# Moving a fused attention and state-space kernel's side work off GpSimd: x in two channel halves, the gate on TensorE, the skip weight in the first tap

## The chip, the cores and the metric

The kernel runs on one core of a Trainium2 chip. The metric is the device time of one execution in microseconds (us). Engines are named as the profile names them: PE (TensorE), ACT (ScalarE), DVE (VectorE), POOL (GpSimd), SP (the queue that issues most DMAs).

## The reference, cut to what matters

```python
x = A_x                                            # (1, 2048, 512), bfloat16
g = sigmoid((x * gate_w).sum(-1, keepdims=True))   # one gate for each row
# a: 32 heads of 16 channels over 2048 rows, softmax attention, then @ wo
# b: for each of 512 channels a causal convolution over 2048 rows with
#    K[d, l] = Re(sum_n C[d,n] * exp(dt*A[d,n])**l * dt*B[d,n]), plus x * Dskip
return g * a + (1 - g) * b
```

Attention needs 32 x 2048 x 2048 exponentials. In the kernel they are 1024 ACT instructions of 128x1024.

## The kernel before: what matters here

A small scheduler writes one fixed program for each engine. The main loop has 512 steps, and a step holds two of the 1024 exponentials (`ET<-SC`). Side work (projections, parameters, the state-space branch) comes from generators that spend a budget of PE and DVE time in each step. **Every engine and the SP queue then run their own list strictly in order**, so an instruction that waits also holds back all that were recorded after it.

```python
for q in range(512):
    ex(2 * q); qk(q + 1); ex(2 * q + 1)     # two exponentials; scores of the next step
    ... pv(q - 1) ...                       # exponentials times V, into OA
    sch.step(rate)                          # side work, as much as the budget allows
```

The stages of the state-space branch share one PSUM bank, `MB`. They run block by block (16 blocks of 32 channels): a table of powers on DVE; K, the first 64 taps; S, the state of every chunk of 64 rows; a scan over the chunks for each quarter of the channels; and y, the output, in 32 units.

```python
def kstage(blk):                             # [...] matmuls PT x weights into MB
    op("DVE", ... Kst(63, ...) <- MB ...)    # ONE Kst
    dma("SP", ... kpd <- Kst ...)
def sstage(blk):                             # after the transposed load Qt<-ptd
    for bank in range(4):
        # 4 matmuls of 128 rows x 64 columns: Ut (x in block form) times Qt, into MB
        op("DVE", ... Sst(512 * (bank % 2), ...) <- MB ...)       # TWO slots
        dma("SP", ... sd <- Sst ...)
def quarter(qr):                             # the scan
    for bl in range(4):
        yield ("AFTER", f"sg{4 * qr + bl}", 4)   # 4 steps after the loads are issued
    # then per chunk: s2 = G*MU; s3 = ...; G = s2 + sg + s3   (all DVE)
def ublocks():                               # x in block form: channel pairs on partitions
    # 8 x  op("POOL", tensor_copy(UB, X2))   64 x 2048 elements each
def gate():
    # 16 x dma xg <- x ;  op("DVE", tensor_tensor_reduce(xg * gw -> gp[lt]))
    # 16 x dma xh <- x ;  op("POOL", xD = xh * Dskip)
for th in (projs(), params(), scan(), bases(), table(), ystage(), ublocks(), gate(), combine(), outs()):
    sch.add(th)                              # priority in this order
```

The softmax here doesn't subtract the row's maximum and nothing guards it: scores larger than these inputs give would overflow.

## Time and profile before

| | before |
|---|---|
| time, median of its runs | 1171.6 us |
| ACT busy | 978.9 us (84%) |
| PE / DVE / POOL busy | 65% / 57% / 6% |
| first exponential | 17.9 us |
| last exponential ends, then tail | 1146.5 us, 22.3 us |

From the page of the kernel before: the busy times, the rows of ACT and of PE's granted clock over 40 slices of the span in tenths, the group of the exponentials, and the group of the POOL copies (busy, mean ns | idle before, and what ended it).

```profile
PE 755.2 (65%) x5997; PEld 204.7 (18%) x6016; DVE 671.8 (57%) x1525; ACT 978.9 (84%) x1039; POOL 64.4 (6%) x36
...
ACT  5456999993798989799879796889799698999992
...
PEclk9767998555556555565655565555555555555568
...
L515 ACT ACTIVATE ET<-SC 128x1024 bf16<-128x1024 f32 x1024 | 965.5, 1104 | 120.0 <-PE SC L422 107.9
...
L926 POOL COPY UB<-X_140 64x2048 bf16<-64x2048 bf16 x8 | 31.4, 3920 | 49.7 <-DMA X_140<-gm_xrd 49.2
```

ACT is the busiest engine. In its timeline, undisturbed stretches run at 0.918 us an exponential (92 in 84.44 us), so 1024 of them need 940 us. The other 229 us of the span are the subject. ACT's row shows them: the first four slices are half empty, many in the middle are at 6 to 8 (one at 3), and the last is at 2. The clock row shows PE at about half clock from about 200 us until near the end (mean 0.85 up to 205 us, 0.52 from there to 1120 us).

The waits view names for each waiter what it waited for: us in total, times, longest.

```profile
ACT ET L515 <- PE SC L422: 107.9, 49, 8.5
...
DVE Sst L778 <- DMA gm_sd<-Sst: 30.5, 12, 4.3
...
DVE G L819 <- DMA SG_136<-gm_sd: 19.5, 2, 17.8
...
ACT ge L945 <- DVE gp L941: 17.6, 1, 17.6
DVE G L819 <- DMA SG_135<-gm_sd: 17.2, 1, 17.2
...
ACT u_101 L607 <- DVE u_99 L540: 9.6, 1, 9.6
ACT u_101 L600 <- DVE u_99 L598: 9.4, 1, 9.4
```

ACT's own line says only that scores came late. Its causes are the lines in which DVE waits for a DMA, because PE needs DVE to empty `MB`, and ACT needs PE. The gate's exponential (`ge`) and the two square roots (`u_101`) waited for DVE directly.

Two stretches of the timeline (start us, duration us, engine, line, what it writes and reads, and in brackets the idle time before it and what ended it). First the head:

```profile
35.62 0.68 DVE L540 TENSOR_TENSOR zi<-u_101,u_102 128x512 f32<-128x512 f32 x1
...
36.74 7.64 POOL L926 COPY UB<-X_140 64x2048 bf16<-64x2048 bf16 x2 [23.95 <-DMA X_140<-gm_xrd]
36.84 4.07 DVE L540 TENSOR_TENSOR u_99<-zr 128x512 f32<-128x512 f32 x1
...
40.84 4.10 DVE L540 TENSOR_TENSOR u_100<-zi 128x512 f32<-128x512 f32 x1
...
46.17 0.63 ACT L600 ACTIVATE u_101<-u_99 128x512 f32<-128x512 f32 x1 [9.39 <-DVE u_99 L598]
```

The same kind of DVE operation takes 0.68 us without a POOL copy beside it and 4.1 us with one. The square root waits 9.4 us for that.

Then a block of the state stage:

```profile
351.40 7.19 SPq L784 DMA_DIRECT2D gm_sd<-Sst  x4
...
355.88 0.42 DVE L778 CAST Sst<-MB 128x256 bf16<-128x256 f32 x1 [4.21 <-DMA gm_sd<-Sst]
...
356.69 0.64 PE L422 MATMUL MB<-Qt,Ut 128*64 128x256 bf16 x4 [4.22 <-DVE Sst L780]
...
357.26 0.61 PE L422 MATMUL SC<-Qm,KT 32*128 32x512 bf16 x4
...
357.91 1.94 ACT L515 ACTIVATE ET<-SC 128x1024 bf16<-128x1024 f32 x2 [4.58 <-PE SC L422]
```

The third `Sst` eviction waits 4.2 us for the store that still reads its slot; then the PE matmuls into `MB` go on, then the scores of the next step, which stand behind them in PE's list, and ACT has been idle for 4.6 us.

### The profile page before, as it was taken

To read this page: it belongs to the slowest core of one execution; us is meant where nothing else is said; L and a number is where in the kernel's file an instruction comes from. 1 tells how busy PE (TensorE), PEld (TensorE's weight loads), DVE (VectorE), ACT (ScalarE), POOL (GpSimd) and SP (SyncE) were. 2 spreads that over 40 slices of the span, in tenths; PEclk is the share of its full clock that TensorE was granted. 3 is DMA by queue.
4 is the path that set the end of the run, shared out by engine and by line. 5 is a ranking of instruction groups with operands and counts; after the bars stand their busy time and mean duration, and the time that the engine had idled before them with its cause. 6 is when DMAs were issued, how large, how long until landed. Compare 5 with 4: busy or idle time off the path is not lost.

```text
span 1168.8 us, 15477 instructions
## 1 busy us (share of the span) xinstructions
PE 755.2 (65%) x5997; PEld 204.7 (18%) x6016; DVE 671.8 (57%) x1525; ACT 978.9 (84%) x1039; POOL 64.4 (6%) x36
## 2 busy tenths in 40 slices
PE   5345766662665656656566775756588467888775
PEld 1111111110111111111111122311133012333111
DVE  5778889965576976589757521129711793011413
ACT  5456999993798989799879796889799698999992
POOL 4442000000000000000000015000000000000000
PEclk9767998555556555565655565555555555555568
DMA  9660000043687018630356635550156203544001
GB/s 217 138 148 36 1 1 1 1 135 99 175 186 189 1 54 199 181 72 1 109 166 163 181 104 141 124 128 1 32 126 122 48 1 93 126 115 112 14 19 49
DMA packets 239176, 111.24 MB, mean 95 GB/s; under 512 B 191616, under 2 KB 222720, under 8 KB 237056
## 3 DMA queue, kind: packets, MB, share of 16 engines
q1 hardware_dynamic: 237376, 108.56, 37.1%
q10 hardware_dynamic: 1728, 1.70, 0.5%
q8 instruction: 47, 0.77, 0.3%
q14 instruction: 25, 0.20, 0.1%
HBM read 42.34 MB, written 39.85 MB: 70 GB/s over the span
## 4 chain that ended last, share of the span: by engine, by line
DVE 35%; ACT 34%; PE 10%; DMA 10%; SPq 6%; issue 2%; POOL 1%; another core or an unknown queue 0%; ACTq 0%; DVEq 0%; POOLq 0%
ACT ET L515 34%; DVE G L829 4%; PE MB L422 4%; DMA gm_sd<-Sst 4%; PE SC L422 4%; DVE s_138 L827 4%; DVE s_138 L822 3%; DVE s_139 L824 3%; PE OA L422 2%; DVE tt_130 L540 2%; DVE PT L540 2%; DMA xg<-in_A_x_dram 2%; DVE tt_131 L540 2%; DVE SG_136 L831 2%; DVE SG_135 L831 2%
## 5 line engine op out<-in xcount | busy, mean ns | idle before, releaser
L515 ACT ACTIVATE ET<-SC 128x1024 bf16<-128x1024 f32 x1024 | 965.5, 1104 | 120.0 <-PE SC L422 107.9
L422 PE MATMUL SC<-Qm,KT 32*128 32x512 bf16 x2048 | 294.9, 566 | 240.4 <-ACT ET L515 225.4
L422 PE MATMUL OA<-ET,VE 128*32 128x512 bf16 x2048 | 292.8, 575 | 13.6 <-DVE OT L530 12.8
L422 PEld LDWEIGHTS SC<-Qm,KT 32*128 32x128 bf16 x2048 | 54.9, 97 | 453.5 <-ACT ET L515 417.9
L890 DVE CAST Yst<-MB 128x256 bf16<-128x256 f32 x32 | 13.4, 420 | 177.0 <-PE MB L422 177.0
L422 PEld LDWEIGHTS OA<-ET,VE 128*32 128x32 bf16 x2048 | 54.0, 101 | 206.9 <-issue 187.0
L422 PE MATMUL MB<-Qt,Ut 128*64 128x256 bf16 x256 | 39.1, 405 | 71.4 <-DVE Sst L780 52.5
L530 DVE STREAM_TRANSPOSE OT<-OA 128x512 f32<-128x512 f32 x32 | 23.8, 744 | 66.9 <-PE OA L422 66.8
L778 DVE CAST Sst<-MB 128x256 bf16<-128x256 f32 x64 | 27.0, 421 | 60.8 <-DMA gm_sd<-Sst 30.5
L829 DVE TENSOR_TENSOR G<-s_138,s_139 128x256 f32<-128x256 f32 x120 | 51.0, 425 | 4.1
L422 PE MATMUL MB<-Tt,Uy 128*64 128x64 bf16 x256 | 33.7, 260 | 29.8 <-DVE Yst L890 15.6
L822 DVE TENSOR_TENSOR s_138<-G,MU 128x256 f32<-128x256 f32 x120 | 50.1, 417 | 0.1
L824 DVE TENSOR_TENSOR s_139<-G,MU 128x256 f32<-128x256 f32 x120 | 50.1, 418 | 0.0
L540 DVE TENSOR_TENSOR PT<-tt_130,tt_131 128x512 bf16<-128x512 bf16 x96 | 40.8, 425 | 3.3
L956 POOL TENSOR_TENSOR xD<-xh,Dsk 128x512 bf16<-128x512 bf16 x16 | 19.6, 1244 | 397.4 <-DMA xh<-in_A_x_dram 397.4
L422 PE MATMUL MB<-xT,Wk 128*128 128x512 bf16 x60 | 21.3, 444 | 26.1 <-DMA xT<-in_A_x_dram 10.4
L926 POOL COPY UB<-X_140 64x2048 bf16<-64x2048 bf16 x8 | 31.4, 3920 | 49.7 <-DMA X_140<-gm_xrd 49.2
L757 DVE CAST Kst<-MB 128x512 bf16<-128x512 f32 x16 | 11.1, 694 | 36.8 <-PE MB L422 36.8
L422 PEld LDWEIGHTS MB<-Tt,Uy 128*64 128x64 bf16 x256 | 16.9, 127 | 83.5 <-issue 67.8
L422 PE MATMUL MB<-Py,SG_136 128*32 128x64 bf16 x512 | 29.9, 314 | 0.0
L422 PE MATMUL MB<-Py,SG_135 128*32 128x64 bf16 x512 | 29.9, 314 | 0.0
L422 PEld LDWEIGHTS MB<-Qt,Ut 128*64 128x64 bf16 x256 | 11.5, 137 | 100.8 <-DVE Sst L780 74.8
(203 smaller groups left out, 647.0 us busy)
## 6 DMA issues: line engine op xcount, KB each, us to landing
gm_ptd<-PT SPq DMA_DIRECT2D x16, 1024.0 KB, 4.0
Py<-gm_ptd SPq DMA_DIRECT2D x32, 512.0 KB, 4.5
gm_sd<-Sst SPq DMA_DIRECT2D x64, 128.0 KB, 1.9
X_140<-gm_xrd SPq DMA_DIRECT2D x8, 512.0 KB, 7.5
gm_ud<-UB SPq DMA_DIRECT2D x4, 1024.0 KB, 5.3
Ut<-gm_ud SPq DMA_DIRECT2D x16, 256.0 KB, 3.4
gm_kpd<-Kst SPq DMA_DIRECT2D x16, 256.0 KB, 3.7
Uy<-gm_ud SPq DMA_DIRECT2D x32, 128.0 KB, 4.3
```

Of the source, the lines that this page charges most:

```text
L422: op("PE", lambda t: t.matmul(out(), lhsT(), rhs(), start=start, stop=stop, skip_group_check=True, **kw), R, W)
L515: op("ACT", lambda a: a.activation(ET(1024 * e, [[1, 1024]]), sc(0, [[1, 1024]]), AF.Exp, scale=DH ** -0.5), [(sc, 0, h // 2), (sc, 1, h / ...
L530: op("DVE", lambda v: v.transpose(OT(o, [[1, 512]]), OA(0, [[1, 512]])), [(OA, 0, b)], [(OT, 0, b)])
L540: op(eng, lambda v: v.tensor_tensor(o(), a(), b_(), f), R, W)
L778: op("DVE", lambda v, bank=bank: v.tensor_copy(Sst(512 * (bank % 2), [[256, 2], [1, 128]]), MB(0, [[256, 2], [1, 128]])), [(MB, 0, ('S', b ...
L822: op(e, lambda v: v.tensor_tensor(s2(0, [[128, 2], [1, 128]]), G(0, [[128, 2], [1, 128]]), MU(d0, [[0, 2], [1, 128]]), ALU.mult), key("G", ...
L824: op(e, lambda v: v.tensor_tensor(s3(0, [[128, 2], [1, 128]]), G(128, [[-128, 2], [1, 128]]), MU(D + d0, [[D, 2], [1, 128]]), ALU.mult), k ...
L827: op(e, lambda v, so=so: v.tensor_tensor(s2(0, [[1, 256]]), s2(0, [[1, 256]]), sg(so, [[1, 256]]), ALU.add), [(s2, 0)] + ks, [(s2, 0)])
L829: op(e, lambda v: v.tensor_tensor(G(0, [[1, 256]]), s2(0, [[1, 256]]), s3(0, [[1, 256]]), ALU.add), [(s2, 0), (s3, 0)], [(G, 0)])
L831: op(e, lambda v, so=so: v.tensor_copy(sg(so, [[1, 256]]), G(0, [[1, 256]])), key("G"), ks)
L926: op("POOL", lambda g, par=par: g.tensor_copy(UB(32 * par, [[64, 64], [1, 32]], 64 * par, 64), X2(par, [[2, 64], [128, 32]], 64 * par, 64) ...
L956: op("POOL", lambda v, lt=lt, r=r: v.tensor_tensor(xD(lt * D, [[1, D]]), B["xh"](r * D, [[1, D]]), Dsk(0, [[1, D]]), ALU.mult), [(B["xh"], ...
```

## The change

Its intent is a loop without GpSimd work. Channels are paired by halves (d with d + 256), so x is loaded straight onto two partition halves and needs no block form. The gate becomes 64 one-column matmuls. The skip weight is added to the first tap in `Kst`. The first 512 rows of x are transposed by PE. Several things come along: the table is built for two blocks at a time, `Sst` gets four slots, y loads run two units ahead, the y stage moves ahead of scan and table in priority, and the square roots are issued four steps later. Further changes that the cut below leaves out are six dummy matmuls before the first ones, weights loaded in pieces, a different order of the first projections and of the first 16 steps' `pv`, and three slots instead of two for the y loads. The core of the diff, cut at the marks:

```diff
-    sb("Sst", 2 * 512)
+    sb("Sst", 4 * 512)
     sb("Kst", 8 * P)
 [...]
+    op("POOL", lambda g: g.iota(idf(0, [[1, P]]), [[1, P]], base=0, channel_multiplier=-1, ...), [], [(idf, 0)])
+    op("POOL", lambda g: g.memset(VE(0, [[1, 16 * 560]]), 1.0), [], [(VE, k) for k in range(16)])
+    op("DVE", lambda v: v.tensor_scalar(idb(0, [[1, P]]), idf(0, [[1, P]]), 0.0, None, ALU.is_equal), [(idf, 0)], [(idb, 0)])
 [...]
+        yield ("Q", p.q + 4)
         op("ACT", lambda a: a.activation(B["u3"](0, [[1, D]]), B["u1"](0, [[1, D]]), AF.Sqrt), key("u1"), key("u3"))
 [...] table():
-        for blk in range(NBLK):
+        for pb in range(NBLK // 2):
+            qr, blks = pb // 2, (2 * pb, 2 * pb + 1)
 [...]
+            if pb:
+                yield ("AFTER", f"K{2 * pb - 1}", 0)
+                yield ("AFTER", f"pt{2 * pb - 1}", 4)
 [...]
+            for i, blk in enumerate(blks):
+                dma("SP", ... ptd <- PT ...)
+                sch.add(qload(blk))
+                sch.add(kstage(blk))
 [...] kstage():
+        op("DVE", lambda v: v.tensor_scalar(Kst(63, [[P, 8]]), MB(0, [[T, 8]]), B["Dp"](blk, [[1, 1]]), None, ALU.add), ...)
 [...] sstage():
-                for p2 in range(2):
-                    mm(... Ut(u0 + 64 * k, [[1, 64]]) x Qt(...), pos=(0, 64 * p2))
+                for j in range(4):
+                    k, par = 4 * bank + 2 * pp + j // 2, j % 2
+                    mm(... X2(2048 * qr + 16 * bl + k, [[64, 32]], 64 * par, 64) x Qt(...), pos=(64 * par, 32 * j))
 [...] ublocks(), gate(): no POOL operations, no xg and xh loads
-    for th in (projs(), params(), scan(), bases(), table(), ystage(), ublocks(), gate(), combine(), outs()):
+    for th in (projs(), gate(), ystage(), params(), scan(), bases(), table(), ublocks(), combine(), outs()):
```

## The prediction

> **What bounds it.** The page: ScalarE (ACT) busy 978.9 of 1168.8 us (84%), PE 65%, DVE 57%, POOL 6%. The 1024 exponentials run back to back at 0.918 us (timeline, 92 in 84.4 us): 940 us is the floor. ACT's timeline shows what is lost beyond it:
> - start: first exponential at 17.9 us;
> - head: 70 exponentials by 132 us, 50 us lost. mostly because DVE's two-input operations of 0.7 to 1.2 us last 3.9 to 4.6 us while a POOL copy (3.9 us) runs, and both square roots make ACT wait 9 us for DVE;
> - gate, 250 to 283 us: DVE waits for x tiles, ACT idles 19 us;
> - state stage, 284 to 690 us: about 50 us in gaps of 2 to 5 us; the waits view has DVE waiting 30.5 us for stores of Sst (two slots), PE and ACT behind it;
> - 690 to 980 us: about 45 us: the DMA queue held by xD tiles (gaps 5.3, 3.4, 5.0), two scans waiting 17 us for transposed loads (8.0, 7.1), two y evictions queued behind a scan (5.2, 5.4);
> - y stage: exponentials at about 1.0 us, PE nearly full at half clock: 20 us;
> - tail: 22 us after the last exponential.
>
> **What the change does.**
> 1. No POOL copies or xD. The Trainium skill ("SBUF — State Buffer", port sharing) says a POOL operation and a two-input DVE operation lock each other out; the 3.9 us operations agree. Table loads (4 x 1.28 us) and some PE-bound first steps remain, about 12 of 50: saves 38.
> 2. Gate on PE: 64 one-column matmuls in slack. Saves 19.
> 3. Sst with four slots, paired table operations: saves 32 of 50. New risk: two transposed loads back to back (4.8 us of queue each), one Kst.
> 4. No xh and Uy loads, y loads two ahead, y before the scan in priority, so y units run during scans 2 and 3: saves 18 of 45; y ends tens of steps earlier, so 12 output projections finish before the last exponential: tail 22 to 13, saves 9.
> 5. First rows by PE transposes instead of a transposing DMA that landed at 10.4 us; parameter work still precedes the first scores. First exponential near 15.5: saves 2.5.
> 6. Costs: S matmuls double (256 to 512), first-tap ones too. Four tiles (64 rows x 32 columns) should run together, as four 128x32 ones do now (0.62 us for four at half clock), so S stays about 0.64 us per bank; y gains two small matmuls per quarter, about 0.1 us per step; estimate 8 us over 128 quarters.
>
> Sum: -38 -19 -32 -18 -9 -2.5 +8, about -111: 1172 - 111, about 1060 us.
>
> **What would show it.** POOL near 1%; no DVE two-input operation over 1.5 us in the head; first exponential at 14 to 17 us, 70th by 95 us; no gate gap; DVE waits for Sst stores near 0; Py matmuls during scans; under 15 us after the last exponential; ACT idle 60 to 90 us instead of 190.
>
> **What would make it wrong.** Higher if 64x32 tiles don't overlap (S and y double their PE time: +20 to +40), if a sustained head brings the half clock (now from about 200 us) into the projections, if Qt or Kst waits replace the Sst ones, or if DVE waiting for scan loads also holds y evictions. The time should lie in 1028 to 1092; faster 0.96, same 0.03, slower 0.01.

## The result and the profile after

The changed kernel took 1103.0 us (median, 1102.0 to 1103.8) against 1171.6 us; the ratio is 0.9413, 95% interval 0.9397 to 0.943. A ratio is the mean time of one kernel's fast runs over that of the other's of the same rounds, so it is not quite the ratio of the medians. The direction was right. The size was not: 68 us instead of 111, and 1103 lies above the stated range of 1028 to 1092.

The same parts of the page of the changed kernel:

```profile
PE 756.7 (69%) x6614; PEld 211.7 (19%) x6614; DVE 634.8 (58%) x1354; ACT 981.1 (89%) x1042; POOL 10.2 (1%) x12
...
ACT  5999999998779987899888959995997999999995
...
PEclk9988985555555556555566655555555555568856
```

POOL is at 1%, ACT's second to fourth slices are full, and the last is at 5. The middle still has sevens and eights, and two fives. PE's half clock begins in the seventh slice, at about 165 us, instead of the eighth, at about 205; the work is further on by then, so it falls in about the same step. The waits view of the changed kernel:

```profile
ACT ET L536 <- PE SC L420: 97.3, 44, 11.6
...
DVE Kst L796 <- DMA gm_kpd<-Kst: 70.4, 8, 15.4
...
PE MB L420 <- DVE Kst L797: 46.6, 8, 11.9
...
DVE G L861 <- DMA SG<-gm_sd: 29.2, 2, 16.8
...
DVE Sst L820 <- DMA gm_sd<-Sst: 4.5, 3, 1.6
```

The waits for `Sst` stores are nearly gone (30.5 us before, 4.5 now), and one that the view of the kernel before has no line for is there: DVE waits 70.4 us for stores of `Kst`.

To place the loss, I took the start of every exponential from ACT's timeline and subtracted 0.918 us for each, between fixed exponentials (step q begins with number 2q). The losses are comparable between kernels because both run the same 1024 exponentials in the same order:

| part, by step | before | after | predicted change | measured change |
|---|---|---|---|---|
| start (first exponential at) | 17.9 | 18.4 | -2.5 | +0.5 |
| head, 0 to 96 | 51.3 | 17.3 | -38 | -34.0 |
| gate, 96 to 112 | 18.6 | 0.1 | -19 | -18.5 |
| state stage, 112 to 304 | 53.5 | 63.8 | -32 | +10.3 |
| rest, 304 to 511.5 | 65.0 | 49.6 | -18 + 8 | -15.4 |
| tail | 22.3 | 12.6 | -9 | -9.7 |
| sum | | | -110.5 | -66.8 |

Two rows have the wrong sign. The state stage alone is off by 42 us, nearly the whole miss. Three stretches of the changed kernel's timeline show what stands there. First, the state stage:

```profile
280.78 4.97 SPq L773 DMA_TRANSPOSE Qt<-gm_ptd  x1
...
281.54 0.66 DVE L796 CAST Kst<-MB 128x512 bf16<-128x512 f32 x1
...
287.56 5.02 SPq L800 DMA_DIRECT2D gm_kpd<-Kst  x2
291.24 0.69 DVE L796 CAST Kst<-MB 128x512 bf16<-128x512 f32 x1 [8.76 <-DMA gm_kpd<-Kst]
...
292.37 0.65 PE L420 MATMUL MB<-Qt,X 64*32 64x256 bf16 x8 [6.55 <-DVE Kst L797]
...
292.95 0.61 PE L420 MATMUL SC<-Qm,KT 32*128 32x512 bf16 x4
...
293.60 3.77 ACT L536 ACTIVATE ET<-SC 128x1024 bf16<-128x1024 f32 x4 [6.25 <-PE SC L420]
```

The first K eviction of a pair (281.54) has its store recorded in SP's list behind transposed loads of `Qt` (280.78) and of chunk states, so it is issued only at 287.56. The second eviction (291.24) needs the same `Kst` and waits 8.8 us. `MB` stays full, PE's next S matmuls (292.37) and the scores behind them (292.95) wait too, and ACT stands idle for 6.3 us.

Second, the start:

```profile
1.08 7.57 POOL L464 MEMSET VE<- 128x8960 bf16 x1
1.18 7.55 DVE L467 TENSOR_SCALAR idb<-idf 128x128 bf16<-128x128 f32 x1
...
8.88 1.86 PE L420 MATMUL SC<-idb,x0n 128*128 128x128 bf16 x16 [4.95 <-DVE piota L471]
...
18.44 1.94 ACT L536 ACTIVATE ET<-SC 128x1024 bf16<-128x1024 f32 x2
```

The identity for the PE transposes, one small DVE operation, takes 7.55 us, as long as the POOL memset that began just before it. The x rows are transposed only at 8.88.

Third, a scan:

```profile
743.69 2.60 SPq L841 DMA_TRANSPOSE SG<-gm_sd  x1
...
748.98 0.29 DVE L861 CAST G<-SG 128x256 f32<-128x256 bf16 x1 [16.78 <-DMA SG<-gm_sd]
...
751.11 0.42 DVE L931 CAST Yst<-MB 128x256 bf16<-128x256 f32 x1
...
751.67 0.28 PE L420 MATMUL MB<-Tt,X 64*32 64x64 bf16 x4 [9.04 <-DVE Yst L931]
...
752.92 6.13 ACT L536 ACTIVATE ET<-SC 128x1024 bf16<-128x1024 f32 x6 [8.76 <-PE SC L420]
```

DVE's first scan copy waits 16.8 us for the transposed loads of the chunk states. The eviction of a y unit (751.11) stands behind it in DVE's list, so PE waits for `MB` and ACT idles 8.8 us.

### The profile page after: what moved, and what is told of

Its sections match the earlier page's. It is cut to its first block, busy times and chain, and to the rows that moved or that the text cites. A ratio compares the mean times of both kernels' runs of the same rounds, so it can differ in the third digit from the quotient of the medians.

```text
span 1102.0 us, 16304 instructions
## 1 busy us (share of the span) xinstructions
PE 756.7 (69%) x6614; PEld 211.7 (19%) x6614; DVE 634.8 (58%) x1354; ACT 981.1 (89%) x1042; POOL 10.2 (1%) x12
## 4 chain that ended last, share of the span: by engine, by line
ACT 43%; DVE 30%; PE 11%; SPq 8%; DMA 5%; issue 2%; ACTq 0%; DVEq 0%; POOL 0%; POOLq 0%
ACT ET L536 42%; PE MB L420 5%; DVE G L871 4%; SPq L773 4%; PE SC L420 4%; DVE s L864 3%; DVE s L866 3%; DVE s L869 3%; DVE SG L873 3%; DMA gm_kpd<-Kst 2%; DVE tt L561 2%; PE OA L420 2%; SPq L841 2%; DMA gm_sd<-Sst 2%; DVE OT L551 1%
## 5 line engine op out<-in xcount | busy, mean ns | idle before, releaser
L536 ACT ACTIVATE ET<-SC 128x1024 bf16<-128x1024 f32 x1024 | 966.2, 1109 | 98.3 <-PE SC L420 97.3
L420 PE MATMUL MB<-Qt,X 64*32 64x256 bf16 x512 | 39.9, 404 | 70.6 <-DVE Kst L797 44.5
L561 DVE TENSOR_TENSOR tt<-B,D 128x1024 bf16<-128x1024 bf16 x96 | 62.0, 688 | 1.3
L420 PE MATMUL MB<-Py,SG 128*32 128x64 bf16 x1024 | 59.8, 314 | 2.3 <-issue 2.3
L796 DVE CAST Kst<-MB 128x512 bf16<-128x512 f32 x16 | 11.0, 689 | 82.5 <-DMA gm_kpd<-Kst 70.4
L871 DVE TENSOR_TENSOR G<-s,s 128x256 f32<-128x256 f32 x120 | 53.2, 444 | 4.1
L420 PE MATMUL MB<-Tt,X 64*32 64x64 bf16 x512 | 35.6, 267 | 27.9 <-DVE Yst L931 27.9
L864 DVE TENSOR_TENSOR s<-G,MU 128x256 f32<-128x256 f32 x120 | 52.8, 440 | 0.1
L866 DVE TENSOR_TENSOR s<-G,MU 128x256 f32<-128x256 f32 x120 | 52.6, 438 | 0.0
L869 DVE TENSOR_TENSOR s<-s,SG 128x256 f32<-128x256 f32 x120 | 51.9, 432 | 0.0
L420 PEld LDWEIGHTS MB<-Py,SG 128*32 128x32 bf16 x1024 | 42.8, 222 | 10.5 <-issue 2.5
L873 DVE CAST SG<-G 128x256 bf16<-128x256 f32 x120 | 36.1, 301 | 4.1
L561 DVE TENSOR_TENSOR ft<-FP,L 128x1024 f32<-128x1024 f32 (+1 forms) x32 | 33.7, 1085 | 0.4
```

Of the source, the lines that this page charges most:

```text
L420: op("PE", lambda t: t.matmul(out(), lhsT(), rhs(), start=start, stop=stop, skip_group_check=True, **kw), R, W)
L536: op("ACT", lambda a: a.activation(ET(1024 * e, [[1, 1024]]), sc(0, [[1, 1024]]), AF.Exp, scale=DH ** -0.5), [(sc, 0, h // 2), (sc, 1, h / ...
L561: op(eng, lambda v: v.tensor_tensor(o(), a(), b_(), f), R, W)
L864: op(e, lambda v: v.tensor_tensor(s2(0, [[128, 2], [1, 128]]), G(0, [[128, 2], [1, 128]]), MU(d0, [[0, 2], [1, 128]]), ALU.mult), key("G", ...
L866: op(e, lambda v: v.tensor_tensor(s3(0, [[128, 2], [1, 128]]), G(128, [[-128, 2], [1, 128]]), MU(D + d0, [[D, 2], [1, 128]]), ALU.mult), k ...
L869: op(e, lambda v, so=so: v.tensor_tensor(s2(0, [[1, 256]]), s2(0, [[1, 256]]), sg(so, [[1, 256]]), ALU.add), [(s2, 0)] + ks, [(s2, 0)])
```

## The experiments

All runs were correct. Each is compared with the kernel before in the same rounds; the changed kernel's ratio to it is 0.9413. "Higher" and "lower" below are differences of these ratios times 1170 us.

### Two Kst slots

```diff
-    sb("Kst", 8 * P)
+    sb("Kst", 2 * 8 * P)
 [...]   # memset, evictions and store likewise
-        op("DVE", ... Kst(63, ...) <- MB ..., [(Kst, 0, blk)])
+        op("DVE", ... Kst(8 * P * (blk % 2) + 63, ...) <- MB ..., [(Kst, blk % 2, blk)])
```

> The changed kernel with two Kst slots instead of one. Theory (the state stage lost its gain to the wait of the second K eviction of a pair on the store of the first): DVE's 70 us of waits for that store fall below 5, ACT's loss in steps 112 to 304 falls from 64 us to 25 to 40, time 1065 to 1080 against 1103. Rival 1 (PE waits for the back-to-back transposed Qt loads anyway): the Kst waits go, but PE waits for Qt in their place, time above 1092. Rival 2 (twice as many S matmuls at half clock): no change, 1098 to 1106.

Measured: 1077.8 us, ratio 0.9223, so 22 us lower. The state stage's loss fell from 63.8 to 33.5 us. The rest, steps 304 to 511.5, rose from 49.6 to 53.9. From its waits view:

```profile
ACT ET L536 <- PE SC L420: 65.7, 44, 9.3
...
DVE G L861 <- DMA SG<-gm_sd: 40.0, 4, 17.3
...
DVE Kst L796 <- PE MB L420: 30.2, 14, 3.2
```

No line of DVE waiting for a `Kst` store is left; it waits for PE there, as it should. ACT's waits fell from 97.3 to 65.7 us. Rivals 1 and 2 fall: had PE stood in the doubled S matmuls or only in the `Qt` loads, this edit would have done nothing; PE's waits for `Qt` are one of 2.4 us. But the waits for the scan's loads rose from 29.2 (2 waits) to 40.0 us (4 waits): two new ones of 5 us, at the scans of the first two quarters inside the state stage. Waits for `Sst` stores also rose, from 4.5 to 12.9 us. Part of the gain passed to the next wait.

### Table built block by block

```diff
-        for pb in range(NBLK // 2):           # two blocks at a time
+        for blk in range(NBLK):               # as before the change
 [...]
-    sb("Sst", 4 * 512)
+    sb("Sst", 3 * 512)                        # four did not fit beside it
```

> The changed kernel with the table built block by block as before (Sst with three slots, not four, so that it fits), Kst still single. Theory (pairing makes the second K eviction follow the first within a few steps): the Kst waits go without a second slot, loss in the state stage 20 to 40 us, time 1065 to 1088 although DVE has some 20 us more table work. Rival 1 (Qt loads back to back): the same, since unpairing spreads them too. Rival 2 (S matmuls): no change, 1098 to 1112.

Measured: 1080.9 us, ratio 0.9253, 19 us lower. The waits for `Kst` stores are gone with a single `Kst`. The loss in the state stage is 47.7 us, above my 20 to 40, and in steps 304 to 440 it fell too (47.7 to 38.0), because the schedule is a different one: the waits for scan loads are 19.3 us. The theory holds (pairing brought the two evictions close enough to meet), but this run changes more than one thing, its total cannot be given to `Kst` alone, and by itself it would not have told the theory from rival 1; the run with two slots does that. Its three `Sst` slots left 12.3 us of waits for `Sst` stores.

### Two Sst slots

```diff
-    sb("Sst", 4 * 512)
+    sb("Sst", 2 * 512)
 [...]   # slot bank % 2 instead of bank
```

> The changed kernel with two Sst slots as before. If the four slots brought what I predicted, the DVE waits for Sst stores come back (about 30 us) and the time rises by 15 to 35 to 1118 to 1138. If the Kst wait had covered them, under 5 more.

Measured: 1127.6 us, ratio 0.9655, 28 us higher. DVE's waits for `Sst` stores are 70.3 us, more than before the change, and the state stage's loss is 88.3 instead of 63.8:

```profile
DVE Sst L820 <- DMA gm_sd<-Sst: 70.3, 17, 13.1
```

So the four slots bring 24.5 us there, net: the waits for `Kst` stores are shorter in this run (43.1 us). The part of my term that I had reasoned about was real; it was more than eaten by the wait that I had not priced.

### Eight POOL copies put back as dummies

```diff
+    op("POOL", tensor_copy(UBd, UBs))   # 8 x 64x2048, meant for steps 2, 10, 18, 26; nobody reads UBd
```

> The changed kernel with the eight GpSimd copies (64x2048) of before put back as dummies into a tile that nobody reads, at the same steps. Theory (the lock between GpSimd and two-input DVE operations cost the head): DVE operations of 0.7 to 1.2 us that meet a copy last 3.9 to 4.6 us again, time up by 15 to 30 to 1118 to 1133. Rival (the head was lost to the delayed x loads and the square roots' order alone): under 4 more.

Measured: 1117.4 us, ratio 0.957, 18 us higher. The loss in steps 0 to 96 rose from 17.3 to 35.7; all other parts stayed within 2.5 us. From its timeline:

```profile
25.63 32.21 POOL L977 COPY UBd<-UBs 64x2048 bf16<-64x2048 bf16 x8 [12.56 <-PE SC L422]
...
29.82 4.11 DVE L563 TENSOR_TENSOR u<-BimT,dt 128x512 f32<-128x512 bf16 x1
33.85 0.68 DVE L504 CAST VE<-MB 128x512 bf16<-128x512 f32 x1
34.45 3.54 DVE L563 TENSOR_TENSOR u<-CreT,u 128x512 f32<-128x512 bf16 x1
```

A two-input operation from SBUF takes 3.5 to 4.1 us beside a copy; the eviction from PSUM between them takes its usual 0.68. The copies did nothing for the result, so their cost is what they do to the other engines: the eight DVE operations that they lengthened took 18.0 us longer than the same ones in the changed kernel, which is the whole loss. But the copies did not run where they were meant to, since they wait for no load as those of before did. All eight ran back to back, from 25.6 to 57.8 us (steps 3 to 10), where the kernel before had four pairs between 36.7 and 93.9 us (steps 7 to 17). So the run shows that the lock exists and that eight copies can cost the head 18 us, not that exactly this much of the 34 us was theirs. An estimate for the kernel before, from its trace: the operations that its copies lengthened took 23 us longer in all than is usual for them (0.69 or 1.22 us).

### Square roots issued at once

```diff
-        yield ("Q", p.q + 4)
         op("ACT", ... AF.Sqrt ...)           # both places
```

> The changed kernel with both square roots issued at once, as before, not four steps later. Theory (a square root issued early makes ACT wait in order for DVE): ACT waits twice for DVE by 2 to 6 us, loss in the head up by 4 to 12 us, time 4 to 12 higher. Rival (the 9 us waits before were only the slow DVE of the GpSimd lock, which is gone): under 3 higher.

Measured: 1114.2 us, ratio 0.9505, 11 us higher, inside the expected range, but not for the expected reason alone. ACT waits only 1.65 and 0.8 us for DVE. The loss up to step 96 is 21.8 instead of 17.3 us; the larger rest lies in steps 96 to 304 (73.9 instead of 63.8), where the whole sequence has moved by a few steps. That part I can't attribute. The four-step delay is worth about 4 us in the head; the 9 us waits before were for a DVE that was late for other reasons: for the first, two operations of 4.1 us beside copies; for the second, one of 3.9 us and 2.5 us of waiting for an x tile of the gate, among others.

### The VE memset after the identity

```diff
-    op("POOL", ... memset(VE, 1.0), [], ...)            # before the identity
+    op("POOL", ... memset(VE, 1.0), [(idb, 0)], ...)    # after it, waits for it
```

> The changed kernel with the 7.6 us GpSimd memset of VE held back until the identity for the PE transposes is made. Theory (the same lock stretched that small DVE operation to 7.6 us and with it the start): the operation takes under 0.5 us, the first exponential comes at 15 to 16.5 us instead of 18.4, time 2 to 3.5 us lower. Rival (the start is bound by the landing of the first x rows or by the issue of ACT's seven loads until 7 us): the first exponential stays at 18 us, change under 1 us.

Measured: 1099.2 us, ratio 0.9378 (0.9353 to 0.9403), about 4 us lower; its interval just overlaps that of the changed kernel, so the profile has to decide:

```profile
1.18 0.23 DVE L466 TENSOR_SCALAR idb<-idf 128x128 bf16<-128x128 f32 x1
...
5.04 1.89 PE L420 MATMUL SC<-idb,x0n 128*128 128x128 bf16 x16 [1.11 <-DMA x0n<-in_A_x_dram]
...
15.37 3.77 ACT L536 ACTIVATE ET<-SC 128x1024 bf16<-128x1024 f32 x4
```

The identity takes 0.23 us, the transposes start at 5.04 when the x rows have landed, and the first exponential comes at 15.4 us instead of 18.4. The prediction's 15.5 was right for the PE transposes; the lock had hidden it.

### The scan nine steps after its loads

```diff
-                yield ("AFTER", f"sg{4 * qr + bl}", 4)
+                yield ("AFTER", f"sg{4 * qr + bl}", 9)
```

> The changed kernel with the scan held back nine steps instead of four after its transposed loads are issued. Theory (DVE's first scan copy stands in its queue waiting up to 17 us for the loads, with the y evictions behind it, so MB stays full and PE and ACT stop: gaps of 8.8 and 7.3 us): the scan's load waits fall from 29 us to under 6, the two gaps vanish, loss in steps 304 to 440 falls from 48 to 30 to 38, time 8 to 15 lower. Rival (those gaps are PE at half clock being full): under 3 lower, or higher because scans start later.

Measured: 1084.6 us, ratio 0.9262, 18 us lower, more than expected. The loss in steps 304 to 440 is 28.0 us instead of 47.7.

```profile
DVE Kst L796 <- DMA gm_kpd<-Kst: 66.6, 8, 14.9
...
DVE G L861 <- DMA SG<-gm_sd: 3.6, 2, 3.2
```

The scan's waits fell from 29.2 to 3.6 us while those for `Kst` stores stayed, so the two causes are separate. Letting the scan come later costs nothing: y units of the previous quarter fill the time.

### The y stage behind scan and table again

```diff
-    for th in (projs(), gate(), ystage(), params(), scan(), bases(), table(), ...):
+    for th in (projs(), gate(), params(), scan(), bases(), table(), ystage(), ...):
```

> The changed kernel with the y stage behind scan and table in priority, as before. Theory (y units running during scans 2 and 3 is what ends y early and shortens the tail): the last y eviction moves from step 443 to 470 or later, the tail after the last exponential grows from 12.6 us to 16 to 22, time 3 to 12 higher. Rival (order of priority does not matter, PE budget alone sets the y stage): within 2 of the changed kernel.

Measured: 1124.6 us, ratio 0.9597, 22 us higher, more than expected. The last y eviction moves from step 443 to 498, only two of the sixteen output tiles are done before the last step, and the tail is 33.7 us instead of 12.6. The mechanism is the expected one; I had underrated the tail.

### The three mends together, and a later S stage

```diff
 # e9_three:      two Kst slots + memset after the identity + scan nine steps after its loads
 # e10_three_qt:  the same, and
-        yield ("AFTER", f"qt{blk}", 3)
+        yield ("AFTER", f"qt{blk}", 5)
```

> The changed kernel with the three mends together: two Kst slots, the VE memset after the identity, the scan nine steps after its loads. Theory (three separate waits, at three different places of the step sequence): the savings of the single runs add up, about 21 + 18 + 4 us, so 1055 to 1066, near the 1060 that I predicted for the change. Rival (one wait only passes its time to the next): 1070 or more.

> As the run before, and each S stage five steps after its transposed load of Qt is issued instead of three. Theory (what is left of the state stage's loss is PE standing in its queue for the second of two transposed loads): PE's gaps of 4 to 5 us before an S stage vanish, 5 to 12 us lower than the run before. Rival (what is left is PE at half clock being full in K and S steps): within 3, or higher because blocks take longer.

Measured: 1048.3 us for the first, ratio 0.8962 (0.8942 to 0.8983); 1046.1 us for the second, 0.8951 (0.8933 to 0.8968). Both beat the kernel before and the changed one. The first is 53 us lower than the changed kernel, better than the sum of the single runs (44). The surplus lies in the state stage, 25.9 us against 33.5 with two `Kst` slots alone: the two waits of 5 us that had appeared at the first two scans are gone there, because the scan now comes later. The first's page:

```profile
PE 758.1 (72%) x6614; PEld 212.0 (20%) x6614; DVE 628.1 (60%) x1354; ACT 978.7 (94%) x1042; POOL 11.1 (1%) x12
```

ACT is busy 94% of the span, yet by the count of the table above 78 us of loss remain (16.3 in the head, 0.1 in the gate, 25.9 and 36.0), beside 14.9 us of start and 12.8 of tail; exponentials that run slowly count as busy too. In the second, the first gap of the state stage shrank from 4.5 to 1.0 us as its theory said and the state stage's loss from 25.9 to 21.7, but the head's rose from 16.3 to 19.2, the time moved by 2 us and the intervals overlap: inconclusive. The other gaps of 3.5 to 3.9 us in the state stage stayed, so what remains there is not mainly the wait for `Qt`.

## Why the prediction was right or wrong

- **Wrong: step 3, "Sst with four slots, paired table operations: saves 32 of 50. New risk: two transposed loads back to back (4.8 us of queue each), one Kst."** The state stage lost 10.3 us more than before instead of 32 less. The slots did save (24.5 us, by the run with two slots). But pairing puts two K evictions a few steps apart, with `Qt` loads between the first one's store and the SP queue's head, and the single `Kst` cost 30 us of that stage (run with two `Kst`). Without that wait the stage lies 20.0 us below before, and 27.6 with the scan later as well (33.5 and 25.9 against 53.5), so the 32 was also somewhat too large; which part of it, the runs do not tell. I named the risk and priced it at nothing. To price it, I would have had to write down the SP queue's order for one pair: two stores of `PT`, two transposed loads of 4.8 us each, and a store of `Kst` that can end up behind either.
- **Wrong by 3 us: step 5, the start.** PE transposes do bring 15.4 us (run with the memset moved), but in the change the identity met the lock between DVE and POOL that step 1 spoke of. I looked for that lock among the operations that were removed, not among those that were added.
- **Right: step 1, the head.** -34 measured, -38 predicted. The lock is the largest part: 18 us by the dummy copies, 23 by the estimate from the trace of before. Delaying the square roots gives about 4. The rest, some 7 to 12 us (x tiles of the gate in DVE's list, order of the first projections and of `pv`, the dummy matmuls), was not tested apart, so the sum is shown and its parts only in part.
- **Right: step 2, the gate.** -18.5 against -19.
- **Right in sum, step 4 and the tail.** Steps 304 on: -15.4 against -10; tail: -9.7 against -9. The early y stage is the cause of the short tail (run with y behind). The risk "DVE waiting for scan loads also holds y evictions" did come true: it cost 18 us (run with the later scan), which the change's other gains hid. That the sum fits is partly luck.
- **Right: step 6, the tiles.** Eight 64x32 matmuls of S take 0.65 us at half clock where four 128x64 ones took 0.64; S as a whole is busy 39.9 us against 39.1. In y, the exponentials' pitch in stretches without scans is 1.012 us before (990 to 1070 us) and 1.020 after (900 to 960), so y cost about 2 us over 256 exponentials and not 8.

The sum was wrong in one term, in a stage where I counted the waits that the change removes and not the places where its new order makes two users of one buffer meet.

## What to carry to other kernels

When a change bunches work (two blocks at a time), walk through the in-order DMA queue for one bunch and look at every buffer with a single slot: the wait moves to the next such buffer. A risk that can be named can be priced from the durations in the trace, and should stand in the sum. Before trusting a gain from taking an engine's work away, look at what that engine does beside the operations that are added; and mend waits together, since one mended alone hands part of its time to the next.

## What the Trainium skill lacked or had wrong

- "SBUF — State Buffer" (Who interferes with whom) says that a DVE instruction in a 2-port mode is blocked for the whole of a GpSimd instruction that was issued first, and that one with two SBUF inputs contends with a GpSimd instruction that reads SBUF. A DVE comparison from fp32 to bf16 took 7.55 us beside a memset of 7.57 and 0.23 us without; two-input operations took up to 4.1 us, instead of 0.68, beside copies of 3.7 to 4.1 us. What the page lacks is the cost to a pipeline: eight such copies lengthened the whole kernel by 18 us although POOL was otherwise idle.
- "TensorEngine Tiling (Array Packing)" (Key Properties) says that tiles operate independently. No page has a time for tiles of 64x32. Here each group of four 64x32 tiles has two on each half of the rows, and eight matmuls of 256 columns took 0.65 us at half clock, the same as four of 128x64.
- "TensorE: Matmul & The Clock Gate" ties the half clock to idle time and its release to activity (What's actually happening), and a peak-current limit to three busy cores of a die (Seeing it yourself). Here, in a kernel on one core, the mean clock was 0.55 from 165 to 1020 us of the changed kernel and 0.52 from 205 to 1120 us of the one before, after 0.93 and 0.85 up to there, and it was 0.50 also where PE was busy 85% of the time (900 to 960 us of the changed kernel). No run here shows why.
- "ScalarE: Activation LUTs" (What ACT_TABLE_LOAD costs) gives 1283 ns for an activation table load and about 1380 ns more for a drain, 2.66 us for every switch. The trace agrees with the first part alone: loads take 1.28 us, and no pause of 1.38 us stands beside one. In the changed kernel an exponential ended at 57.70 us, the load began at 57.71 and the square root at 59.00.
- "TensorE: Matmul & The Clock Gate" (Architectural detail) calls VectorE's queue strict FIFO, and nothing here contradicts it. In the changed kernel the matmuls of a y unit ended at 741.26 us, and its eviction ran only at 751.11, behind a scan copy that had waited 16.8 us for its load.
